# Attention with beacon keys and an ELU feed-forward on one Trainium2 core: a planner's order replaced by tables of order, engines and buffers, with batch 0's keys and queries loaded in two parts

## The chip, the cores and the metric

The kernel runs on one core of a Trainium2 chip. Its engines are TensorE (matrix products; PE in the profile, PEld for its weight loads), VectorE (DVE), ScalarE (ACT), GpSimd (POOL) and SyncE (SP, which only issues DMAs here). Each engine works through its own list of instructions in order and waits on semaphores for what other engines or DMAs have finished. The metric is device microseconds of one execution: the median of 3 runs before is 353.73 us (353.72 to 354.24).

## The reference

For 8 batches and 8 heads, with 576 queries of 64 elements, 16 beacon keys and values that every query sees, and a causal mask over the 576 others; then a feed-forward with ELU over all 4608 tokens:

```python
k_all = concatenate([beacon_k, k], axis=2);  v_all = concatenate([beacon_v, v], axis=2)
scores = matmul(q, k_all.T) / sqrt(64);      scores = where(causal, -1e9, scores)
a = exp(scores - max);                       a /= a.sum(-1) + 1e-09
x = matmul(a, v_all)                         # back to (4608, 512)
h = x @ w_in                                 # 512 -> 2048
g = where(h > 0, h, exp(min(h, 0)) - 1)
out = g @ w_out                              # 2048 -> 512
```

## The kernel before, in words

**Attention.** Heads are taken in pairs (4 pairs a batch, 32 in all). Keys and queries must stand with their 64 elements on the partitions. For batches 0 to 2 a pair's keys and queries are loaded together (L314, 288 KB each), cast to bf16 in one instruction (L323) and transposed by TensorE in ten 128 x 128 pieces (L388, L390; batch 0: L398, L401, into two buffers). Copies then put them in order into kT and qT (L413, L415, L411; L422, L423, L428). Batches 3 to 7 are loaded by token (L340), cast (L346) and transposed by DMA (L353). The scores of a pair are computed in four units (L439), each unit one exponential on ScalarE (L448) with masks by GpSimd on the diagonal pieces (L454). The products with the values (L473) carry a column of ones, whose sum divides the result (L488, L489). The result is turned into xT by TensorE (L499, copy L510) for batches 0 and 1 and by DMA (L359) from batch 2 on.

**Feed-forward.** Tokens go in 11 tiles: 128, 128, 256, then eight of 512. Up: four accumulating matmuls for each 512 columns of output (L529), exponential on ScalarE (L536), clamp on GpSimd (L540), join with max on VectorE (L549). Down: sixteen accumulating matmuls for 128 tokens (L563), a copy (L569), a store (L573). The last 128 tokens are written in two halves. The weights are loaded by GpSimd with a cast on the way (L380), one quarter of a matrix in each DMA.

**Buffers.** PSUM holds two score buffers of two banks (tag sc) and four banks (tag ff) for all else; SBUF has 6 staging buffers of loads (4 of them until batch 1's keys are turned), 3 of casts (2 until then), 8 of exponentials, 18 of feed-forward activations.

**What sets the order.** A planner (class Plan, L27) runs a small model of the engines while the kernel is built: every operation has an engine, a priority key, a duration and the buffers it takes and gives back; at each moment the free engine takes the ready operation with the lowest key for which buffers are there. Keys come from tuned numbers (SHIFT, AT, AT0, PACES and others). Until 30 us of its model, whenever TensorE has nothing ready, the planner puts in a filler: a matmul of ones into a spare bank (L274), which keeps TensorE running. The order found is then written out, so on the chip it is fixed; the fillers are counted out beforehand. A filler's buffer comes from a rotating pool, so most fillers wait for an earlier filler. ScalarE issues 56 loads (half of the token loads, most values), SP the others, all transposes by DMA and the stores; GpSimd issues the 8 loads of weights. The next DMA on SP or ScalarE takes one of 8 semaphores in turn and waits for that one's earlier transfer.

The functions that the change and the prediction touch:

Of the kernel before, what the change touches and what calls it, by code (L numbers as in the profile page):

```python
# [15 lines left out]
P = 128  # L16


class Op:
    def __init__(self, eng, key, dur, fn, deps=(), take=(), give=(), mode=None, lat=0.03, queue=0, parts=1):  # L20
        self.eng, self.key, self.dur, self.fn = eng, key, dur, fn
        self.deps, self.take, self.give = [d for d in deps if d is not None], take, give
        self.mode, self.lat, self.queue, self.parts = mode, lat, queue, parts
        self.left, self.after, self.rest = 0, [], parts


class Plan:  # L27
    MODE_COST = 0.1

    def __init__(self, slots, window):  # L30
        self.slots, self.window, self.ops = dict(slots), window, []

    def add(self, *args, **kw):
        op = Op(*args, **kw)
        self.ops.append(op)
        return op

    def run(self):
        for i, op in enumerate(self.ops):
            op.seq = i  # L40
            op.left = len(op.deps)
            for d in op.deps:
                d.after.append(op)
        ready = {op.eng: [] for op in self.ops}
        pending = {eng: sorted((o.key, o.seq) for o in self.ops if o.eng == eng) for eng in ready}
        done = set()
        first = dict.fromkeys(pending, 0)
        free = dict.fromkeys(pending, 0.0)
        mode, lines, turn = None, ([], [], []), 0

        def arrive(o):
            if o.eng == "DMA":
                lines[o.queue].append(o)
            else:
                heapq.heappush(ready[o.eng], (o.key, o.seq))

        for op in self.ops:
            if not op.left:
                arrive(op)
        events, order, now, n_left, tick = [], [], 0.0, len(self.ops), 0  # L60
        while n_left:
            for eng in ready:
                if free[eng] > now + 1e-9:
                    continue
                if eng == "DMA":
                    if any(lines):
                        turn = next((turn + i) % 3 for i in (1, 2, 3) if lines[(turn + i) % 3])
                        op = lines[turn][0]
                        free[eng] = now + op.dur / op.parts
                        heapq.heappush(events, (free[eng], tick, None))  # L70
                        tick += 1
                        op.rest -= 1
                        if not op.rest:
                            lines[turn].pop(0)
                            heapq.heappush(events, (free[eng] + op.lat, tick, op))
                            tick += 1
                    continue
                line = pending[eng]
                while first[eng] < len(line) and line[first[eng]][1] in done:
                    first[eng] += 1  # L80
                if first[eng] == len(line):
                    continue
                limit = line[first[eng]][0] + self.window.get(eng, 1e9)
                skipped, op = [], None
                while ready[eng]:
                    item = heapq.heappop(ready[eng])
                    o = self.ops[item[1]]
                    if item[0] > limit:
                        skipped.append(item)
# [788 lines left out]
```

## Time and profile before

| what | value |
|---|---|
| median of 3 runs | 353.73 us |
| the profiled execution: span from the first to the last instruction | 352.5 us |
| TensorE busy | 343.3 us (97%), of which fillers 19.1 |
| VectorE, ScalarE, GpSimd busy | 205.8, 194.1, 179.4 us |
| DMA | 52.55 MB, mean 149 GB/s |
| first score matmul, first up-projection matmul | 9.38 us, 31.91 us |

The profile comes from one execution, and its span is 1.2 us under the median of the runs; sums are made against the span. "Busy" of TensorE counts fillers too, and its matmuls overlap each other: where the pace matters, take the difference between two starts. A DMA share above 1 says that packets overlap within the 16 transfer engines.

### The profile page before, as it was taken

Reading aid. Unit: us, or ns where it says so; the run is one execution under the profiler, and the core shown is the slowest. Engines: PE = TensorE matmul, PEld = TensorE weight load, DVE = VectorE, ACT = ScalarE, POOL = GpSimd, SP = SyncE. Lnnn points to the kernel's source line nnn. Section 1 sums busy time; section 2 is a strip of 40 time slices with the busy share of each in tenths; the row PEclk is TensorE's granted clock in tenths of the full one; section 3 lists DMA queues with packets and bytes.
Section 4 is the critical chain, followed back from the end, with each engine's and each line's share of the span. In section 5 each row is a group of like instructions: output and inputs, shape, how many; then the busy total and the mean of one; then the engine's idle time right before and its main releaser. Section 6 shows DMA issues by size and latency. Waiting matters only on the chain.

```text
span 352.5 us, 8440 instructions
## 1 busy us (share of the span) xinstructions
PE 343.3 (97%) x3295; PEld 195.6 (55%) x3295; DVE 205.8 (58%) x428; ACT 194.1 (55%) x289; POOL 179.4 (51%) x353
## 2 busy tenths in 40 slices
PE   8999999999999989999999999999999999999996
PEld 5668887545555445545476664554445544444444
DVE  1478797557556567557746565764665555455322
ACT  2586887577556746684576547663477443343200
POOL 5587776556635655475475455463554333434200
PEclk9999999999999999999999999999999999999999
DMA  7999996798998979899999679767460220000112
GB/s 189 260 286 221 206 238 130 227 215 146 165 209 144 208 153 185 160 195 204 152 232 150 146 138 237 143 104 182 96 144 32 60 69 32 31 31 32 47 72 91
DMA packets 139480, 52.55 MB, mean 149 GB/s; under 512 B 127536, under 2 KB 131888, under 8 KB 139440
## 3 DMA queue, kind: packets, MB, share of 16 engines
q1 hardware_dynamic: 87472, 35.55, 46.7%
q10 hardware_dynamic: 47744, 12.26, 18.9%
q0 software_dynamic: 4224, 4.19, 7.1%
q8 instruction: 26, 0.43, 0.5%
q14 instruction: 14, 0.11, 0.1%
HBM read 37.22 MB, written 9.44 MB: 132 GB/s over the span
## 4 chain that ended last, share of the span: by engine, by line
PE 82%; DMA 7%; DVE 4%; SPq 2%; POOL 1%; issue 1%; ACT 1%; ACTq 0%; POOLq 0%; DVEq 0%
PE ops L563 32%; PE hps L529 32%; PE av L473 8%; PE sc L439 7%; DMA st<-in_k_dram 3%; PE spare L274 3%; DMA st<-in_q_dram 2%; DMA xT<-x 1%; SPq L314 1%; DMA kT<-st 1%; DVE gt L549 1%; POOL et L454 1%; DVE x L489 1%; ACT et L448 1%; POOL e L540 1%
## 5 line engine op out<-in xcount | busy, mean ns | idle before, releaser
L529 PE MATMUL hps<-xT,w_in 128*128 128x512 f16 (+2 forms) x768 | 141.4, 326 | 2.8 <-DVE gt L549 1.3
L563 PE MATMUL ops<-w_out,gt 128*128 128x512 f16 (+1 forms) x592 | 143.9, 374 | 0.0
L549 DVE SCALAR_TENSOR_TENSOR gt<-e,hps 128x512 f16<-128x512 f32 x144 | 97.6, 684 | 74.9 <-POOL e L540 74.5
L540 POOL TENSOR_SCALAR e<-e 128x512 f32<-128x512 f32 x144 | 88.1, 614 | 102.4 <-ACT e L536 100.5
L536 ACT ACTIVATE e<-hps 128x512 f32<-128x512 f32 x144 | 85.6, 600 | 94.3 <-PE hps L529 90.2
L448 ACT ACTIVATE et<-sc 128x768 f16<-128x768 f32 (+3 forms) x128 | 104.1, 863 | 31.8 <-PE sc L439 31.6
L529 PEld LDWEIGHTS <-w_in 128*128 128x128 f16 x768 | 68.0, 98 | 57.6 <-issue 3.6
L563 PEld LDWEIGHTS <-gt 128*128 128x128 f16 x592 | 54.1, 98 | 56.5 <-issue 3.0
L454 POOL TENSOR_SCALAR_AFFINE_SELECT et<-et 128x256 f16<-128x256 f16 (+2 forms) x160 | 61.5, 410 | 44.9 <-ACT et L448 40.8
L473 PEld LDWEIGHTS <-et 128*128 128x128 f16 (+1 forms) x960 | 36.1, 97 | 11.0 <-issue 2.2
L569 DVE COPY osb<-ops 128x512 f32<-128x512 f32 (+1 forms) x37 | 25.0, 675 | 26.2 <-PE ops L563 25.3
L473 PE MATMUL av<-v,et 128*128 128x65 f16 (+1 forms) x960 | 39.7, 193 | 0.3 <-DVE x L489 0.3
L439 PE MATMUL sc<-qT,kT 64*128 64x80 bf16 (+3 forms) x704 | 35.2, 228 | 0.3 <-ACT qT L428 0.2
L489 DVE TENSOR_TENSOR x<-av,rl 128x256 f16<-128x256 f32 (+2 forms) x68 | 32.1, 472 | 2.3
L439 PEld LDWEIGHTS <-kT 64*128 64x128 bf16 x704 | 20.7, 95 | 18.9 <-issue 16.8
L488 DVE RECIPROCAL rl<-av 128x4 f32<-128x4 f32 (+2 forms) x68 | 12.4, 182 | 21.4 <-PE av L473 20.3
L373 DVE CAST v<-vst 128x512 f16<-128x512 f32 (+1 forms) x40 | 21.1, 529 | 4.1 <-DMA vst<-in_v_dram 4.1
L274 PE MATMUL spare<-ones 128*128 128x256 bf16 x111 | 19.1, 304 | 1.6 <-DVE ones L816 1.3
L274 PEld LDWEIGHTS <-ones 128*128 128x128 bf16 x111 | 10.9, 109 | 6.2 <-issue 1.7
L346 DVE CAST st<-st 128x1024 bf16<-128x1024 f32 (+2 forms) x18 | 11.6, 655 | 2.8 <-DMA st<-in_k_dram 1.4
L323 POOL CAST st<-st 128x1152 bf16<-128x1152 f32 x8 | 9.1, 1142 | 5.7 <-DMA st<-in_q_dram 3.9
L346 POOL CAST st<-st 128x1024 bf16<-128x1024 f32 (+2 forms) x12 | 10.7, 892 | 2.0 <-DMA st<-in_k_dram 2.0
(35 smaller groups left out, 68.0 us busy)
## 6 DMA issues: line engine op xcount, KB each, us to landing
out_dram<-osb SPq DMA_DIRECT2D x35, 256.0 KB, 2.6
st<-in_q_dram ACTq DMA_DIRECT2D x20, 256.0 KB, 4.3
vst<-in_v_dram ACTq DMA_DIRECT2D x15, 256.0 KB, 4.1
st<-in_k_dram SPq DMA_DIRECT2D x15, 256.0 KB, 5.0
st<-in_k_dram SPq DMA_DIRECT2D x12, 288.0 KB, 7.1
st<-in_q_dram SPq DMA_DIRECT2D x11, 288.0 KB, 6.9
vst<-in_v_dram SPq DMA_DIRECT2D x9, 256.0 KB, 7.0
w_in<-in_moe_w_in_dram POOLq DMA_DIRECT2D x4, 512.0 KB, 12.7
```

Source lines behind the costliest of these rows:

```text
L274: nc.tensor.matmul(out=spare[:, 0:2 * P], lhsT=ones[:, 0:P], rhs=ones, start=True, stop=True)
L439: nc.tensor.matmul(out=sc[:, h, o:o + w], lhsT=kT[D * h:D * h + D, P * jc:P * jc + P], rhs=qT[D * h:D * h + D, q0:q0 + w], start=True, sto ...
L448: nc.scalar.activation(out=et[:, :, 0:w], in_=scs[n, u][:, :, 0:w], func=AFT.Exp, bias=0.0, scale=float(1.0 / (D ** 0.5)))
L454: nc.gpsimd.affine_select(out=et[:, :, c0:c0 + dw], in_=et[:, :, c0:c0 + dw], compare_op=ALU.is_ge, fill=fill0, base=q0 + NB - P * jc, pat ...
L473: nc.tensor.matmul(out=av[:, c:c + D + 1], lhsT=ets[n, CUT.unit_of[jc, at]][0:m, h, col:col + P], rhs=v16[0:m, jc, 2 * hp + h, 0:D + 1], s ...
L489: nc.vector.tensor_tensor(out=x16s[b % 2][:, blks[0]:blks[0] + nb, P * hp:P * hp + P].rearrange("q i (h d) -> q i h d", d=D), in0=av[:, :, ...
L529: nc.tensor.matmul(out=hps[:, o:o + z - a], lhsT=w_in16[:, cc, P * fc:P * fc + P], rhs=xT[cc][:, a % RING:a % RING + z - a], start=(cc == ...
L536: nc.scalar.activation(out=e, in_=hpss[tt, i], func=AFT.Exp, bias=0.0, scale=1.0)
L540: nc.gpsimd.tensor_scalar(out=e, in0=e, scalar1=1.0, scalar2=0.0, op0=ALU.min, op1=ALU.max)
L549: nc.vector.scalar_tensor_tensor(out=gt, in0=es[tt, i], scalar=1.0, in1=hpss[tt, i], op0=ALU.subtract, op1=ALU.max)
L563: nc.tensor.matmul(out=opss[tt, t4][:, cols], lhsT=gts[tt, fc][:, P * t4:P * (t4 + 1)], rhs=w_out16[:, fc, cols], start=(fc == 0), stop=(f ...
L569: nc.vector.tensor_copy(out=osb[:, slice(*cols)], in_=opss[tt, t4][:, slice(*cols)])
```

## The change

The planner goes. A class Program holds the operations with the engines that each may use and the buffers that each takes and gives back, and three tables say the rest: ORDER, one number for each operation in the order in which they are written out (negative numbers stand for that many fillers); PICKS, a letter for each operation that may run on several engines; PLACES, which buffer each taken one is. Buffers are fixed tiles instead of rotating pools. The tables were made outside the kernel by a planner that took transfers on time and late at once.

Batch 0's keys and queries are loaded, cast, transposed and copied in two parts, tokens 0 to 255 and 256 to 575; the first unit of scores needs only the first part. A unit of scores is one operation (before, two were tied together in most places). The memsets of the beacon buffers and of the exponentials' pads go to VectorE. Which engine casts and copies, and which queue issues a load, is decided by PICKS: ScalarE issues 22 loads instead of 56, SP 233 DMAs instead of 191, GpSimd 8 as before. In the built programs there are 76 fillers instead of 111, the first 15 ahead of the first transpose (before 28).

```diff
-class Plan:
...
-                if op is None:
-                    if eng == "PE" and now < self.fill_until and self.slots["ff"]:
...
+    def run(self, order, picks, places, fill):
+        picks, places, used = iter(picks), iter(places), set()
+        for op in self.ops:
+            if len(op.engines) > 1:
+                op.eng = next(picks)
...
+        for i in order:
+            if i < 0:
+                at = int(next(places), 36)
+                assert ("bank", at) not in used
+                fill(self.rooms["bank"][at])
+                continue
+            op = self.ops[i]
...
+ORDER = [i for t in """
+0 1 12 13 14 90 20 19 -15 15 16 17 18 21 -9 22 26 97 98 51 91 58 52 53 27 23 24 25 -7 30 92 4 32 33 34 35 -1 93
...
+    rooms = {
+        "st": tiles(6, [P, 2, G * D], FP32, "st"),
+        "sb": tiles(3, [P, G, 2, D], BF16, "sb"),
...
+        "bank": [psum.tile([P, 512], FP32, name=f"bank_{i}") for i in range(4)],
+        "pair": [psum.tile([P, 2, 512], FP32, name=f"pair_{i}") for i in range(2)],
...
+    CUTS = (0, 256, S)
+    GS = [(z - a) // HALF for a, z in zip(CUTS, CUTS[1:])]
...
+    def add_pair_halves(n):
...
+        for half in range(2):
+            if half == 0:
+                k_in = st = add("SA", load_k, n, half, take=["st"])
...
+            T = add("P", do_T2, n, half, deps=[cast] + (all_T[b][-1:] if half else [bk_in[b]]), take=["bank"],
+                    give=[(sb, 0)] if half else [])
...
+            need = ready if b else ready[0] + (ready[1] if u else [])
+            SC = add("P", do_SC, n, u, deps=need, take=["pair"])
...
-            nc.gpsimd.memset(t, 0.0)
-            nc.gpsimd.memset(et[:, :, CUT.width[-1]:CUT.width[-1] + P - BLOCKS[-1][1]], 0.0)
+        nc.vector.memset(t, 0.0)
+        nc.vector.memset(et[:, :, WIDTH[-1]:WIDTH[-1] + P - BLOCKS[-1][1]], 0.0)
```

More of the change, by code (lines that the diff above doesn't have):

```diff
@@ L1 @@
-import heapq
-from functools import partial
 from contextlib import ExitStack
@@ L173 @@
     assert G * HALF == S
+    CUTS = (0, 256, S)
+    GS = [(z - a) // HALF for a, z in zip(CUTS, CUTS[1:])]
+    VG = 4
     NKC = -(-SK // P)
@@ new lines, in do_P, with do_Pcopy @@
+    def do_P(e, bank0, bank1, b, half):
+        for g in range(VG):
+            for c, bank in ((2 * half, bank0), (2 * half + 1, bank1)):
+                vps[b, c] = bank
+                rows = slice(32 * c, 32 * c + 32)
+                e.matmul(
+                    out=bank, lhsT=sel[rows, g, :], rhs=vq[rows, :, D * g:D * g + D],
+                    start=(g == 0), stop=(g == VG - 1), skip_group_check=True)
+    def do_Pcopy(e, b, c):
+        copy(e, v16s[b % 2][:, c, :, 0:D], vps[b, c].rearrange("p (h d) -> p h d", h=H))
```

1139 lines of the change are left out of this document (489 added, 650 removed), and 70 rows, old and new, of the table ORDER.

## The prediction

> **What bounds the kernel now.** I read the page first, then the windows, the groups by line, TensorE's timeline and the chain. The page says that TensorE is the engine, and the groups of its lines say how much of that is not work of the reference: the fillers of L274.
>
> ```profile
> PE 343.3 (97%) x3295; PEld 195.6 (55%) x3295; DVE 205.8 (58%) x428; ACT 194.1 (55%) x289; POOL 179.4 (51%) x353
> ...
> L274 PE MATMUL spare<-ones 128*128 128x256 bf16 x111 | 19.1, 304 | 1.6 <-DVE ones L816 1.3
> ```
>
> The span is 352.5. So a planner that only packs TensorE tighter has 352.5 - 343.3 = 9.2 us of idle time and 19.1 us of fillers to win. Where they lie is seen in the windows (columns: stretch and its length, busy us of PE, PEld, DVE, ACT and POOL with counts, granted clock, DMA share, GB/s); 31.9 is the start of the first up-projection matmul:
>
> ```profile
> 0.00:31.90 31.90, 28.91 (x364) 20.91 (x365) 16.36 (x54) 17.58 (x26) 22.10 (x50) 1.00 1.08 238
> 31.90:60.00 28.10, 27.82 (x458) 23.44 (x458) 22.95 (x54) 22.34 (x35) 19.72 (x38) 1.00 1.10 210
> 60.00:260.00 200.00, 197.23 (x1901) 107.21 (x1899) 122.88 (x247) 121.05 (x179) 107.04 (x211) 1.00 0.90 172
> 260.00:352.50 92.50, 89.34 (x578) 44.08 (x576) 43.60 (x75) 33.10 (x52) 30.50 (x56) 1.00 0.16 50
> ```
>
> Idle time of TensorE: 2.99 us up to 31.9, 0.28 to 60, 2.77 to 260, 3.16 to the end, which is the last copy and store. In the built order all fillers stand ahead of 31.9. The first stretch is therefore the only large one: of its 31.9 us, 31.9 - 2.99 - 19.1 = 9.8 us are work. TensorE's timeline (start, length, operation, count) shows its two ends and the pace of the fillers:
>
> ```profile
> 1.26 5.70 PE L274 MATMUL spare<-ones 128*128 128x256 bf16 x28 [1.26 <-DVE ones L816]
> 7.00 0.68 PE L398 MATMUL tr<-identb,st 128*128 128x128 bf16 x9
> ...
> 13.95 2.25 PE L274 MATMUL spare<-ones 128*128 128x256 bf16 x19
> 16.04 0.34 PE L473 MATMUL av<-v,et 128*128 128x65 f16 x6
> ...
> 31.91 1.05 PE L529 MATMUL hps<-xT,w_in 128*128 128x128 f16 x16 [0.54 <-DVE xT L510]
> ```
>
> Twenty-eight fillers took 7.00 - 1.26 = 5.74 us, 0.205 each; later nineteen took 16.04 - 13.95 = 2.09, 0.11 each. After 60 TensorE waits for little; the view of the waits (who for whom, us in total, times, longest) has two rows worth naming, and the chain (start, length, what) shows one of them to begin with a late transfer:
>
> ```profile
> PE hps L529 <- DVE gt L549: 1.3, 2, 0.9
> PE hps L529 <- DMA xT<-x: 0.8, 1, 0.8
> ```
>
> ```profile
> 126.41 3.38 DMA kT<-st
> ...
> 131.45 1.89 PE hps L529 x8
> ```
>
> **The change, part by part.** The work of TensorE is the same: both built programs hold the same matmuls except 76 fillers for 111. The question is the place of the first up-projection and what follows it.
>
> *Fillers and the first stretch.* In the built order of the changed kernel the first L529 group (now L547) stands behind the same 9.8 us of work, behind 72 fillers, and behind 30 changes between score matmuls (64 rows) and others; before there were all 111 fillers and 24 changes. A change of kind costs time:
>
> ```profile
> 157.23 0.81 PE L529 MATMUL hps<-xT,w_in 128*128 128x512 f16 x3
> 157.97 0.52 PE L439 MATMUL sc<-qT,kT 64*128 64x256 bf16 x14
> 158.42 1.04 PE L529 MATMUL hps<-xT,w_in 128*128 128x512 f16 x4
> 159.29 1.03 PE L563 MATMUL ops<-w_out,gt 128*128 128x512 f16 x4
> ```
>
> Four matmuls of 512 columns take 159.29 - 158.42 = 0.87, so three take 0.65; with scores behind them the three took 157.97 - 157.23 = 0.74. I take 0.09 us for each change, into the scores and out of them. Six more are +0.55.
>
> The fillers: 15 stand ahead of the first transpose, 15 x 0.205 = 3.1, and 57 later. At the bare pace these are 57 x 0.11 = 6.3; at the mean of the later 83 before, (19.1 - 5.74) / 83 = 0.161 with their waits in them, 9.2. So the fillers take 9.4 to 12.3 us, and if the idle 2.99 us stay, the first up-projection starts at 9.8 + 0.55 + 2.99 + 9.4 = 22.7 to 25.6. The lower end supposes that every wait falls as the table planned it. I take 25.0, nearer the upper end, since transfers that come late turn into idle time where fillers are counted out beforehand: 31.9 - 25.0 = **-6.9 us**.
>
> Can the other engines follow? ScalarE must get through 16 exponentials of batch 0 ahead of that point; VectorE and GpSimd feed it; w_in must have landed.
>
> ```profile
> L448 ACT ACTIVATE et<-sc 128x768 f16<-128x768 f32 (+3 forms) x128 | 104.1, 863 | 31.8 <-PE sc L439 31.6
> ...
> L454 POOL TENSOR_SCALAR_AFFINE_SELECT et<-et 128x256 f16<-128x256 f16 (+2 forms) x160 | 61.5, 410 | 44.9 <-ACT et L448 40.8
> ```
>
> ```profile
> 9.76 0.78 ACT L448 ACTIVATE et<-sc 128x736 f16<-128x736 f32 x1 [1.17 <-PE sc L439]
> 22.66 3.20 POOL L380 DMA_DIRECT2D w_in<-in_moe_w_in_dram x4
> ```
>
> ```profile
> DMA to landing us min/median/max: 8.2/12.7/17.1
> ```
>
> The last row is of w_in. 16 x 0.863 = 13.8 us from the first exponential, and about 2 us of copies that the new order puts between them. The first exponential began at 9.76, behind a load of 288 KB for each of keys and queries, a cast and a transpose at 7.00. In parts, 4 of 9 columns come first: the cast and the copies shrink with them, and 15 fillers ahead of the transpose (1.26 + 3.1 = 4.4) say when the table wants it. With the first exponential at about 7.3 the last ends at 7.3 + 13.8 + 2 = 23.1 or later. So 22.7 is about the floor, and 25.0 can be kept. The first w_in is issued on GpSimd behind four casts and eight masks instead of at 22.66; eight masks of 0.41 chained behind exponentials put it near 14, and with 8.2 to 12.7 to landing it is there at 22 to 27. This is what is late next: if it is 27, the gain is 4.9.
>
> *The loads in parts.* Eight more DMAs in all, and 42 more on SP's queue: ScalarE issues 22 instead of 56. The bytes are the same. That the pieces of 1024 and 1280 bytes cost the transfer engines more than those of 2304 no row shows; bounded by nothing and by one doubling of the share of batch 0's keys and queries, I take nothing, since the stretch after keeps 1.10 of DMA share anyway and the table has the order of loads in its hand.
>
> *Preparing tiles.* Ten memsets move from GpSimd to VectorE, which had nothing between its own memsets and 7.49:
>
> ```profile
> L823 POOL MEMSET et<- 128x96 f16 x8 | 1.0, 178 | 0.0
> L820 POOL MEMSET bk<- 128x512 bf16 x2 | 1.0, 524 | 0.0
> ```
>
> ```profile
> 7.49 0.49 DVE L413 COPY kT<-tr 128x320 bf16<-128x320 bf16 x1 [5.89 <-PE tr L398]
> ```
>
> Hidden by that wait for the first loads; without the cover 2 us at most, once.
>
> *After the first up-projection.* 148 changes of kind in all for 136; six more lie here: +0.55. Of the 2.77 + 0.28 us of idle time, the 0.8 behind DMA xT<-x and the wait ended at 131.45, which starts with a key transpose, are what a plan with late transfers should lose; bounds -2.8 (all gone) and +3.0 (three more waits like the longest, 0.9). I take **-1.0**.
>
> *The end.* The last group is the same halved tile, one copy and store: 3.16 us, no change.
>
> Sum: -6.9 + 0.55 - 1.0 = -7.35, with the other +0.55 already inside the 25.0. The span goes from 352.5 to 345.15; the median of the runs, 353.73, is 1.2 above this span, so 346.4.
>
> *The clock.* The row of the 28 fillers at 0.205 and that of the 19 at 0.11 are two paces of one instruction; if the paces are 0.21 and 0.11, the slow one held for most of the 28, some 5 us. With 15 fillers ahead of the first transposes, up to ten of the later ones may still be slow: +1.0, which is inside the 25.0. A rule speaks against the change here: the Trainium skill, "TensorE: Matmul & The Clock Gate", Part 1, says that TensorE starts at 1.2 GHz, gets 2.4 GHz after about 3.4 us of sustained work, and falls back after an idle window of that length. By the Trainium skill's 3.4 us the +1.0 would be next to nothing, if no gap comes ahead of the first transpose; the trace's 5 us is longer.
>
> **Rivals.**
> 1. *The table holds to its plan.* Fillers at the bare pace, first up-projection at 22.7, all later waits gone: 352.5 - 9.2 + 0.55 - 2.8 = 341.05, so 342.3. Against it: before, too, 111 fillers at the bare pace (28 x 0.205 + 83 x 0.11 = 14.9) became 19.1.
> 2. *The transfers take it back.* The DMA share stands at 1.08 and 1.10 up to 60 us, so it is full; if weights and batch 1 land when they did, TensorE waits for them and the early start is worth nothing: 352.5 + 1.1 - 1.0 = 352.6, so 353.8, no change. For it: the full share. Against it: TensorE waited only 0.28 us from 31.9 to 60, so the loads were ahead of it.
> 3. *SP's queue becomes single file* (the other side). 42 more loads stand on the queue that also issues the transposes:
>
> ```profile
> L353 SPq DMA_TRANSPOSE kT<-st x25: 1174/1211/2362, 77.3 to 247.1; - x25
> L353 SPq DMA_TRANSPOSE qT<-st x25: 1188/1217/2577, 81.7 to 250.9; - x25
> ```
>
> ```profile
> L359 SPq DMA_TRANSPOSE xT<-x x30: 1183/1251/2437, 101.8 to 285.7; - x30
> ```
>
> ```profile
> 23.75 0.34 SPq L369 DMA_DIRECT2D vst<-in_v_dram x1
> 24.14 1.26 SPq L314 DMA_DIRECT2D st<-in_k_dram x2
> ```
>
>    At 0.34 to 0.63 us each, 42 loads are 14 to 26 us more on SP. Each waits in line for a landing or a free buffer, and behind it wait the transposes of batches 2 to 7 and the stores. If all of it delays a transpose that TensorE needs, the cost is 14 or more: 345.15 + 14 = 359.15, so 360.4. It decides from 7.35 / 6 = 1.2 us a batch. Against it: 80 transposes of 1.2 us are 98 us and the 153 other DMAs 52 to 96, together 150 to 194 of the first 290 us, so SP has room on the mean.
> 4. *The clock stays low.* A wait that no filler covers keeps the slow pace: the 9.8 us of work and the 57 later fillers (6.3) take twice as long, 25.0 + 16 = 41 for the first up-projection, so 352.5 + 9.1 + 0.55 - 1.0 = 361.2 and 362.4. Against it: no wait of TensorE in any row here is over 1.3 us, and the pace, once 0.11, stayed so. The fall back after idle time in the Trainium skill, "TensorE: Matmul & The Clock Gate", Part 1, would make this case; no row here shows one.
>
> **How the numbers follow.** Forecast 0.77, its own range from just above rival 1 to 351.0 (25.6 and +3.0 instead of 25.0 and -1.0: 352.5 - 6.3 + 0.55 + 3.0 = 349.75, so 351.0). Rival 1 0.06, rival 2 0.06, rival 3 0.09, rival 4 0.02. The range of 8 in 10 is 342.3 to 351.0: it holds the forecast and half of rival 1. A measurement of this kernel tells about 0.2% (0.7 us) from no change. Faster: 0.77 + 0.06 = 0.83. Same: 0.06. Slower: 0.09 + 0.02 = 0.11.
>
> **What would show it.** The first L547 matmul near 25; fillers at 10 to 12 us busy; idle time of TensorE from there to 260 at 2 us or less; SP without a wait that ends in TensorE. I am wrong if the first up-projection starts after 28, if TensorE idles more than 4 us between it and 260 behind DMA or behind what a transpose feeds, or if the filler pace is 0.2 after the first transpose.

## The result and the profile after

The changed kernel takes 357.86 us (median of 4 runs, 357.00 to 359.35), the kernel before in the same session 353.90 (353.72 to 354.24): a ratio of 1.0127 (95% interval 1.009 to 1.0165). It is 1.3% slower; the forecast was 346.4. The profiled execution took 358.2, its span is 356.5, 4.0 more than before.

The page (share of the span, instructions) and the group of the fillers:

```profile
PE 342.4 (96%) x3260; PEld 192.3 (54%) x3260; DVE 206.8 (58%) x439; ACT 187.0 (52%) x283; POOL 180.2 (51%) x352
...
L294 PE MATMUL bank<-ones 128*128 128x256 bf16 x76 | 15.2, 321 | 1.3 <-DVE ones L768 1.3
```

TensorE is busy 0.9 us less than before, and its idle time went from 9.2 to 14.1. The windows of the changed kernel, in the same stretches (the last with its own end), say where:

```profile
0.00:31.90 31.90, 28.18 (x387) 19.82 (x388) 20.99 (x79) 17.97 (x26) 17.01 (x39) 1.00 0.96 232
31.90:60.00 28.10, 26.09 (x406) 21.38 (x404) 21.38 (x43) 20.52 (x32) 22.25 (x41) 1.00 1.05 211
60.00:260.00 200.00, 195.32 (x1857) 105.06 (x1856) 116.62 (x234) 110.92 (x167) 104.37 (x205) 1.00 0.93 171
260.00:356.50 96.50, 92.81 (x620) 46.02 (x618) 47.83 (x85) 37.55 (x61) 36.58 (x70) 1.00 0.16 51
```

Idle time is the length less the first number behind it: 2.01 us from 31.9 to 60 (before 0.28), 4.68 to 260 (before 2.77), 3.69 at the end (before 3.16). TensorE's timeline of the start (start, length, operation; in brackets the idle time ahead and what ended it):

```profile
1.26 3.38 PE L294 MATMUL bank<-ones 128*128 128x256 bf16 x15 [1.26 <-DVE ones L768]
6.19 0.61 PE L354 MATMUL bank<-identb,sb 128*128 128x128 bf16 x4 [1.55 <-DVE sb L291]
...
6.70 2.13 PE L294 MATMUL bank<-ones 128*128 128x256 bf16 x9
8.62 0.74 PE L354 MATMUL bank<-identb,sb 128*128 128x128 bf16 x5
9.29 0.49 PE L465 MATMUL pair<-qT,kT 64*128 64x240 bf16 x4
...
28.20 1.07 PE L547 MATMUL bank<-xT,w_in 128*128 128x128 f16 x16
```

The first up-projection starts at 28.20 instead of 31.91. So the start did gain, 3.7 us, and the stretch behind it lost more. In the chain of the changed kernel (start, length, what) the up-projection begins with the landing of the first quarter of w_in, at 28.16:

```profile
18.03 10.13 DMA w_in<-in_moe_w_in_dram
```

TensorE's own list had come there at 28.10, so it waited only 0.1 us for it. In other profiles this wait is longer (see the experiments).

To add up the losses I took, for each matmul, the distance to the next one's start, less the bare pace of its shape (0.216 us for 512 columns, 0.109 for 256, 0.056 for 128) and 0.095 for each change into or out of scores. What is left is waiting, over all of it; the idle times above are smaller, since they leave out the part of a wait in which the matmul ahead is still counted as running. Behind the first up-projection it sums to 5.1 us before and to **11.7** after. Of the 11.7, 1.74 lie at 45 us in one place, 6.0 between 120 and 220 (before 2.0), 0.7 in the last 6 us (before nothing).

The places are seen in single rows. At 45 us TensorE waits for an exponential, which waits for a copy of keys on VectorE; VectorE's rows show four joins of the feed-forward ahead of that copy (its transposes ended at 43.1):

```profile
42.24 2.47 DVE L565 SCALAR_TENSOR_TENSOR gt<-e,bank 128x512 f16<-128x512 f32 x4
44.63 0.82 DVE L291 COPY kT<-pair 128x576 bf16<-128x576 bf16 x2
```

```profile
46.95 0.51 PE L465 MATMUL pair<-qT,kT 64*128 64x240 bf16 x14 [1.68 <-ACT et L474]
```

At 150 us a copy into an output buffer waits for a store that frees the buffer. SyncE's rows (SPq) show the stores behind four transposes:

```profile
139.83 5.13 SPq L515 DMA_TRANSPOSE xT<-x  x4
145.00 0.58 SPq L595 DMA_DIRECT2D out_dram<-osb  x1
145.63 0.43 SPq L395 DMA_DIRECT2D st<-in_k_dram  x1
146.16 0.63 SPq L595 DMA_DIRECT2D out_dram<-osb  x1
```

```profile
149.93 0.69 DVE L591 COPY osb<-bank 128x512 f32<-128x512 f32 x1 [1.36 <-DMA out_dram<-osb]
```

```profile
150.68 1.67 PE L547 MATMUL bank<-xT,w_in 128*128 128x512 f16 x7 [0.98 <-DVE osb L591]
```

And SyncE as a whole: summing the lengths of its DMA rows between 120 and 220 us gives 71.2 us in 68 DMAs before and **94.0 us in 91 DMAs** after, 41 of them transposes in both. At their median lengths (1.26 us a transpose, 0.58 a load or store) the 91 would make 81 us; the other 13 are rows that take longer, and what those wait for the rows don't say. No pause between two of these rows is longer than 0.5 us after; before there are pauses of 3.5, 3.4 and 4.1. Before 120 and behind 220 the two kernels are alike (40.9 and 40.1 from 60 to 120; 29.2 and 28.1 from 220 to 260).

### The profile page after: what moved, and what is told of

Same layout as the page of the kernel before. It is cut to its first block, busy times and chain, and to the rows that moved or that the text cites. A ratio compares the mean times of both kernels' runs of the same rounds, so it can differ in the third digit from the quotient of the medians.

```text
span 356.5 us, 8356 instructions
## 1 busy us (share of the span) xinstructions
PE 342.4 (96%) x3260; PEld 192.3 (54%) x3260; DVE 206.8 (58%) x439; ACT 187.0 (52%) x283; POOL 180.2 (51%) x352
## 4 chain that ended last, share of the span: by engine, by line
PE 65%; DMA 12%; DVE 8%; POOL 7%; SPq 3%; issue 3%; ACT 2%; DVEq 0%; ACTq 0%; POOLq 0%
PE bank L585 30%; PE bank L547 23%; PE bank L495 5%; PE pair L465 5%; DVE gt L565 3%; POOL e L558 3%; DMA w_in<-in_moe_w_in_dram 3%; POOL et L479 3%; DMA w_out<-in_moe_w_out_dram 2%; DMA qT<-sb 2%; DMA st<-in_k_dram 2%; DVE kT L291 1%; ACT et L474 1%; DMA st<-in_q_dram 1%; DVE osb L591 1%
## 5 line engine op out<-in xcount | busy, mean ns | idle before, releaser
L474 ACT ACTIVATE et<-pair 128x800 f16<-128x800 f32 (+3 forms) x128 | 105.6, 867 | 66.6 <-PE pair L465 64.0
L547 PE MATMUL bank<-xT,w_in 128*128 128x512 f16 (+2 forms) x768 | 136.0, 326 | 3.1 <-DVE osb L591 2.0
L585 PE MATMUL bank<-w_out,gt 128*128 128x512 f16 (+1 forms) x592 | 133.7, 373 | 1.6 <-DVE gt L565 0.6
L565 DVE SCALAR_TENSOR_TENSOR gt<-e,bank 128x512 f16<-128x512 f32 x144 | 95.7, 683 | 59.5 <-POOL e L558 58.8
L554 ACT ACTIVATE e<-bank 128x512 f32<-128x512 f32 x144 | 83.3, 602 | 75.5 <-PE bank L547 65.2
L591 DVE COPY osb<-bank 128x512 f32<-128x512 f32 (+1 forms) x37 | 25.0, 675 | 55.0 <-PE bank L585 32.7
L495 PE MATMUL bank<-v,et 128*128 128x65 f16 (+1 forms) x960 | 38.6, 193 | 0.8 <-POOL et L479 0.3
L465 PE MATMUL pair<-qT,kT 64*128 64x80 bf16 (+3 forms) x704 | 36.2, 229 | 2.3 <-ACT et L474 2.0
L509 DVE TENSOR_TENSOR x<-bank,rl 128x256 f16<-128x256 f32 (+2 forms) x68 | 32.1, 471 | 2.3
L508 DVE RECIPROCAL rl<-bank 128x4 f32<-128x4 f32 (+2 forms) x68 | 12.4, 182 | 15.9 <-PE bank L495 15.3
L294 PE MATMUL bank<-ones 128*128 128x256 bf16 x76 | 15.2, 321 | 1.3 <-DVE ones L768 1.3
```

Of the source, the lines that this page charges most:

```text
L294: nc.tensor.matmul(out=bank[:, 0:2 * P], lhsT=ones[:, 0:P], rhs=ones, start=True, stop=True)
L465: e.matmul(out=pair[:, h, o:o + w], lhsT=kT[D * h:D * h + D, P * jc:P * jc + P], rhs=qT[D * h:D * h + D, q0:q0 + w], start=True, stop=True ...
L474: e.activation(out=et[:, :, 0:w], in_=scs[n, u][:, :, 0:w], func=AFT.Exp, bias=0.0, scale=float(1.0 / (D ** 0.5)))
L495: e.matmul(out=av[:, c:c + D + 1], lhsT=ets[n, unit_of[jc, at]][0:m, h, col:col + P], rhs=v16s[b % 2][0:m, jc, 2 * hp + h, 0:D + 1], start ...
L509: e.tensor_tensor(out=x16s[b % 2][:, blks[0]:blks[0] + nb, P * hp:P * hp + P].rearrange("q i (h d) -> q i h d", d=D), in0=av[:, :, :, 0:D] ...
L547: e.matmul(out=bank[:, o:o + z - a], lhsT=w_in16[:, cc, P * fc:P * fc + P], rhs=xTa[:, cc, a % RING:a % RING + z - a], start=(cc == 0), st ...
```

## The experiments

Three theories: **A**, SyncE's single file makes transposes, loads and stores late (rival 3 of the prediction, smaller); **B**, the fixed order puts on VectorE or GpSimd an operation that TensorE doesn't need ahead of one that it does; **C**, the weights or what else the start waits for are late. All edits are on the changed kernel. The table has each kernel's median, its ratio to the kernel before (interval), and from its one profile the start of the first up-projection, the waits from 120 to 220 us and all waits behind the first up-projection, counted as above. The medians come from several sessions, so the ratios are what to compare.

| kernel | us | ratio | first up-projection | waits 120-220 | all later waits |
|---|---|---|---|---|---|
| changed | 357.86 | 1.0127 (1.009-1.0165) | 28.20 | 6.0 | 11.7 |
| e1_osb4 | 358.12 | 1.0094 (1.006-1.0127) | 28.34 | 5.1 | 10.5 |
| e2_stores_first | 376.75 | 1.0661 (1.0562-1.0761) | 27.87 | 6.0 | 28.8 |
| e3_w_in_early | 361.29 | 1.0187 (1.0108-1.0266) | 29.72 | 5.0 | 10.8 |
| e4_loads_act | 366.18 | 1.0322 (1.024-1.0403) | 30.24 | 5.8 | 19.4 |
| e5_fill24 | 360.86 | 1.018 (1.0126-1.0234) | 28.12 | 9.3 | 15.3 |
| e7_order | 356.01 | 1.0034 (1.0004-1.0065) | 29.93 | 6.1 | 9.7 |
| e9_score_first | 358.19 | 1.0102 (1.0032-1.0172) | 30.32 | 6.0 | 12.6 |
| e10_stores_pool | 362.61 | 1.0224 (1.0187-1.0262) | 30.15 | 2.9 | 13.1 |
| e11_casts | 355.21 | 1.0027 (0.9998-1.0056) | 28.99 | 5.1 | 9.3 |
| e12_stores_act | 352.60 | 0.9956 (0.9933-0.9978) | 29.28 | 1.5 | 5.5 |
| e13_both | 352.18 | 0.9961 (0.9937-0.9985) | 27.61 | 3.1 | 7.3 |
| e14_fill_gap | 350.96 | 0.9928 (0.99-0.9956) | 27.58 | 1.3 | 4.6 |
| e15_stores_act_alone | 356.28 | 1.0041 (1.0009-1.0073) | 29.59 | 1.5 | 8.1 |
| e16_gap_alone | 358.17 | 1.0115 (1.0064-1.0166) | 27.62 | 5.4 | 12.4 |
| e17_vector_relief | 359.91 | 1.0156 (1.0112-1.02) | 30.67 | 5.3 | 11.5 |

The first up-projection is itself not steady: in the ten profiles whose edits don't touch what stands ahead of it (changed, e1, e2, e4, e7, e10 to e13, e15) it lies between 27.61 and 30.24. In each of them TensorE's list has come to it 0.1 to 1.5 us earlier, and the landing of the first quarter of w_in ends the wait. In e7:

```profile
27.97 0.43 PE L529 MATMUL bank<-identh,x 80*128 80x80 f16 x5
29.93 1.07 PE L552 MATMUL bank<-xT,w_in 128*128 128x128 f16 x16 [1.54 <-DMA w_in<-in_moe_w_in_dram]
```

So waits are compared place by place, times by the ratios, and a shift of the start by less than 2.6 us in one profile says little.

### SyncE's single file

**e1**: a fourth output buffer, the one freed longest ago taken next.

```diff
-        "osb": tiles(3, [P, DM], FP32, "osb"),
+        "osb": tiles(4, [P, DM], FP32, "osb"),
+                if room == "osb":
+                    at = self.spare.pop(0)
```

> The changed kernel with four output buffers instead of three, taken in the order in which they came free. Theory A (SP's single file: stores stand behind transposes, and VectorE waits for an output buffer): VectorE's three idle stretches of 7.3 us ahead of L591 go, and with them TensorE's waits of about 2.9 us near 148, 150, 184 and 187; the time falls from 357.9 to 354.5 to 355.5. Theory B (VectorE, GpSimd and ScalarE have casts and copies ahead of joins in their fixed lists, SP does not decide): the waits stay, 357 to 358.5. Theory C (weights late at the start) expects 357 to 358.5 as well.

The time did not fall by the 2.4 to 3.4 us of theory A. The waits at 148 to 150 and 184 went as far as they hung on output buffers, but new ones came: at 157 (0.83) behind a cast that waits for its load, at 207 (1.38) behind a transpose, and at 196 (1.01) behind a cast whose own wait the profile doesn't explain. So the buffer was one place where lateness showed, and not what made it.

**e2**: each store is issued directly behind its copy.

```diff
+    for i, op in enumerate(plan.ops):
+        if op.fn is do_store:
+            order.insert(order.index(i - 1) + 1, i)
```

> The changed kernel with each store put in the order directly behind its copy, so ahead of the transposes that stood between. Theory A: as with a fourth buffer, 354.5 to 355.5, unless a store at the head of SP's list holds back the transposes while it waits for its copy; then up to 358. Theory B and C: 357 to 358.5.

The time is 6.6% above the kernel before. SyncE stands at the store until the copy is done, and loads and transposes stand behind it; the view of the waits has SyncE waiting for these copies:

```profile
SPq L595 <- DVE osb L591: 116.3, 20, 24.8
```

This is 116.3 us in 20 waits, where the changed kernel has 82.0 in 13. So the table was right to set stores late, and a DMA that waits on SyncE costs what stands behind it. The same kernel shows the clock: behind a gap of 4.62 us four matmuls of 512 columns take 1.86 instead of 1.03 us (granted clock 0.53 from 96 to 103.3):

```profile
93.12 1.03 PE L547 MATMUL bank<-xT,w_in 128*128 128x512 f16 x4
98.77 1.86 PE L547 MATMUL bank<-xT,w_in 128*128 128x512 f16 x4 [4.62 <-DVE osb L591]
```

**e10**: all stores on GpSimd's queue, in their places.

```diff
-                    add("S", do_store, p, t4, c0, c1, deps=[o], give=[(o, 0)])
+                    add("G", do_store, p, t4, c0, c1, deps=[o], give=[(o, 0)])
```

> The change, with all stores issued from GpSimd's queue in the places that the table has for them, instead of SyncE's; 37 DMAs of 0.78 us by the rows of its weight loads, 29 us on an engine that is busy for 180 of 356. Theory A (stores and transposes in one file): the waits at 148 to 150, 159 and 184 go (2.9 of the 11.7) and loads issue earlier; the time falls by 1 to 3 us where GpSimd has room. Theory B (order on the engines): those go, but clamps and masks behind the stores' issue wait 0.8 us each time, 37 times; new waits of 0.2 to 0.5 at the places where a clamp is next: the late waits stay at 10 to 16 and the time at 357 to 362.

From 120 to 220 the waits fell from 6.0 to 2.9, as theory A has it. But at 101 GpSimd stood 2.78 us at a store whose copy was late, and masks stood behind it (TensorE waits 1.55); and at 263 TensorE waits 2.3 us for a copy whose output buffer a store frees that GpSimd, behind masks, had issued only at 261.92. The file was moved to another engine.

```profile
101.67 0.58 POOL L595 DMA_DIRECT2D out_dram<-osb  x1 [2.78 <-DVE osb L591]
102.27 0.75 POOL L479 TENSOR_SCALAR_AFFINE_SELECT et<-et 128x256 f16<-128x256 f16 x2
```

**e4**: query loads of batches 3 to 7 and value loads of 3 to 6 on ScalarE, where the kernel before has many of them.

```diff
+                if op.fn.__name__ in ("load_tok", "load_tok2") and not op.args[1] or op.fn.__name__ == "load_v" and op.args[0] in (3, 4, 5, 6):
+                    op.eng = "A"
```

> The changed kernel with the query loads of batches 3 to 7 and the value loads of batches 3 to 6 on ScalarE's queue, as before the change; the order is kept. Theory A: SP has about 35 DMAs fewer ahead of stores and transposes, the 7.3 us stretches of VectorE shrink, 354 to 356. Theory B: no gain, 357 to 358.5, or slower, up to 361, where a load that waits for a buffer holds back ScalarE's exponentials.

It is worse than either theory had it. A load that stands behind ScalarE's exponentials is issued when ScalarE gets there; in the chain one is issued at 85.6 and lands 6.91 later, at 92.55. VectorE has stood at its cast for 4.30 us, and the copy that frees a bank for TensorE stands behind the cast:

```profile
92.64 0.42 DVE L403 CAST sb<-st 64x512 bf16<-64x512 f32 x1 [4.30 <-DMA st<-in_q_dram]
92.98 0.68 DVE L593 COPY osb<-bank 128x512 f32<-128x512 f32 x1
```

```profile
93.71 1.70 PE bank L549 x4
```

**e15**: only stores that ScalarE need not wait for go to ScalarE: 13 of the 37, those that the table puts several ScalarE operations behind their copy. Nothing else.

```diff
+LATE = [1023, 1001, 1149, 1143, 1155, 1231, 1243, 1237, 1325, 1331, 1319, 1401, 1407]
...
+        for i in LATE:
+            self.ops[i].eng = "A"
```

> The changed kernel with the 13 late stores issued by ScalarE instead of SyncE, and nothing else. Theory A (SyncE's single file holds most of the later waits from 120 to 215): of the 11.7 us of late waits the 6.2 from 120 to 220 fall to 2 or less, those at 45 (1.74), 49 to 94 (2.0) and 350 (0.68) stay; late waits 7 to 8 us, the time 3.5 to 5 us less than the change's 357.9, ratio about 1.000. Theory B (order on VectorE and GpSimd, for which the moved stores only helped together with the repaired order): late waits stay above 9.5.

As theory A expected: 8.1 us of waits in all, 1.5 from 120 to 220. The window of that stretch, changed kernel and then e15:

```profile
120.00:220.00 100.00, 96.16 (x948) 54.49 (x946) 59.63 (x119) 56.65 (x87) 53.49 (x106) 1.00 0.95 179
```

```profile
120.00:220.00 100.00, 99.52 (x990) 56.59 (x988) 63.67 (x127) 59.94 (x93) 55.70 (x110) 1.00 1.10 189
```

TensorE's idle time there is 3.84 us and 0.48 (1.25 in the kernel before); the DMA share rises from 0.95 to 1.10, so the transfers had room. By the ratios the time is 0.9% less than the changed kernel's, some 3 us, a little under the 3.5 to 5 expected. That the start of this profile is 1.4 us later is not the reason: e7 starts at 29.93 and keeps 6.1 us of waits in this stretch, e14 starts at 27.58 and has 1.3. SyncE's rows still fill 90.7 us, with 7 DMAs fewer inside, but there are pauses again (1.0 us at 208, 5.6 at 217). So a small relief was enough; why so little is enough, no run shows.

### The order on the engines

The edits of e7, e9, e11 and e16 move operations while the kernel is built; where a diff shows numbers of operations, it is the order before and behind the edit, and not the code.

**e7** (on e1): VectorE's copy of keys ahead of two joins; at the end, the last tile's first half ahead of the last quarter of the tile before, so that its copy has matmuls beside it.

```diff
-1032 1033 1034 1035 984 985 986 987 261 262 263
+1032 1033 1034 984 985 986 261 262 1035 987 263
...
-1763 1764 1766 1767 1768 1770 1771 1772
+1766 1767 1768 1763 1764 1770 1771 1772
```

> The kernel with four output buffers, and two places of the table put in another order: the key copy of batch 1's last pair ahead of two joins on VectorE (43.4 instead of 44.6), and at the end the last tile's first half ahead of the fourth quarter of the tile before, so that its copy lies beside matmuls. Theory B (a fixed order on VectorE that stands an op which TensorE needs behind two that it doesn't): the wait of 1.74 us at 45 becomes 0.4 to 0.8, the wait of 0.68 at 350 goes, the rest stays; time 1.5 to 2.0 us under that with four output buffers (358.1 beside a before of 354.8), so a ratio of 1.004 to 1.006. Theory A (SyncE's single file is the whole of it): these two places change, but what follows waits that much longer for transfers: no more than 0.5 us is left of it by 260 us.

The wait of 1.74 became 0.55 and that at the end went. In the profile of e7 the same scores as at 46.95 above:

```profile
47.48 0.51 PE L470 MATMUL pair<-qT,kT 64*128 64x240 bf16 x14 [0.49 <-ACT et L479]
```

The two places are worth 1.9 us of waits, and they were theory B's. The stretch from 120 to 220 kept its 6.1.

**e11** (on e7): two token casts, which stood on VectorE ahead of joins while their loads were late, put behind those joins, and two transposes of keys behind two of xT.

```diff
-1155 639 649 640 641 642 511 1260 1261 1262 1263 612 1248 1244 1245 1246 586 587
+1155 649 511 1260 1261 1262 1263 612 1248 1244 1245 1246 586 587 639 640 641 642
...
+    move([760], behind=1363)
+    move([762, 761, 763], behind=737)
```

> The kernel with the two places put in another order (four output buffers), and two token casts on VectorE, which stood ahead of joins while their loads were late (157 and 196), put behind those joins; the second one's two key transposes on SyncE go behind the two transposes of xT that TensorE waited for at 208. Theory B (order on VectorE): the waits at 158 (0.80) and 196 (1.02) go, and that at 208 (1.95) falls below 0.5; late waits 9.7 to 6 to 7, time 3 us less than the kernel it starts from, beside its start as it falls (28.2 or 30). Theory A (SyncE is always busy from 118 to 215 and every load and transpose is as late as before): the waits move to the next load or transpose; late waits stay at 8.5 to 10.

The waits named went or shrank (208: 1.95 became two of 0.32 and 1.25), and others came in their place: 1.55 at 151, where the next cast on VectorE waits for its load, and 0.85 at 227. 9.3 us for 9.7, and the ratio is the same as e7's: theory A.

```profile
151.46 0.69 DVE L406 CAST sb<-st 128x1024 bf16<-128x1024 f32 x1 [2.63 <-DMA st<-in_k_dram]
```

**e12** (on e7): the 13 stores of e15 on ScalarE.

> The kernel with the two places put in another order, and 13 of the 37 stores issued by ScalarE instead of SyncE, those that the table sets 7 or more ScalarE operations behind their copy, so that ScalarE need not wait for them. SyncE loses 13 issues of 0.6 us, 8 us between 100 and 260. Theory A (single file): loads and transposes from 118 to 215 come up to 6 us earlier by the end of it, the waits at 123, 132 to 134, 158, 185, 196 and 208 (5.6 in all) fall below 2.5; ScalarE pays 13 x 0.4 beside its 187 us. Theory B: they stay at 4.5 or more.

The waits from 120 to 220 fell to 1.5, all later waits from 9.7 to 5.5, about what the kernel before has, and the ratio is 0.9956: faster than before.

**e13**: e11 and e12 in one.

> Both: the casts behind the joins and the 13 stores on ScalarE. If the two causes are separate, late waits fall to 4 to 5 us (before has 5.1), and with the start at 28.2 the span is 348 to 350; ratio 0.985 to 0.995. If one makes the other needless, late waits as in the better of the two.

7.3 us of waits, not 4 to 5; one of them, 1.0 at 55, is the landing of w_out. The casts add nothing that shows once SyncE is relieved.

### The start

**e3**: the first load of w_in is issued ahead of the later casts on GpSimd (operation 972 behind the cast of pair 1's first part).

> The changed kernel with the first quarter of w_in issued by GpSimd ahead of the masks and the value cast, so at about 9 to 10 us instead of 18. Theory C (the start is set by the landing of w_in at 28.2): the first up-projection moves from 28.2 to 25.5 to 26.5 and the time falls by about 2 to 355.5 to 356.5. If later waits absorb what the start wins (theory A or B alone), the first up-projection moves and the time stays at 357 to 358.5.

The first up-projection came at 29.72, not earlier, and TensorE has no wait for w_in ahead of it any more. The chain of this kernel goes through a value load that took 8 us:

```profile
10.58 8.00 DMA vst<-in_v_dram
```

So an earlier w_in alone brings nothing in this profile: TensorE's list comes to the up-projection late. Part of that is the clock (granted 0.88 from 10 to 30 us, in the changed kernel 1.00), so this isn't a clean test. For the changed kernel itself theory C is worth the 0.1 us that TensorE waits for w_in there, and in the other profiles up to 1.5.

**e5**: the fillers behind the first 24 are left out (they compute nothing that is used).

```diff
+        n += i < 0
+        if i >= 0 or n <= 24:
+            order.append(i)
```

> The change, with its 52 fillers behind the first 24 left out (they compute nothing that is used). Theory S1 (the start is set by the chain of loads, casts, copies and exps; fillers only fill it): the first up-projection stays at 28.2 +- 0.5, TensorE idle before it grows by the time of those fillers (6 to 8 us), the late waits stay at 11.7, time 357 to 360 unless the clock falls. Theory S2 (fillers stand ahead of work that is ready, since the table planned them for later loads): the first up-projection comes 1 to 4 us earlier and the time falls to 354 to 357. Rival on the clock: with gaps of several us the matmuls behind them run at twice their pace for some 4 us, as behind the gaps of the kernel with each store behind its copy; then the first up-projection comes later than 28.7.

The first up-projection stayed at 28.12. From 1.26 us to there TensorE's idle time grew from 2.3 to 5.7 us, and the granted clock fell from 1.00 to 0.87 (0.83 from 9.3 to 20 us). So the fillers fill time in which little else is ready, as S1 has it, and they keep the clock up; a gain that the lower clock took back isn't excluded by this profile. Later the kernel had more waits (9.3 from 120 to 220).

**e9**: the first unit of scores ahead of the second half's transposes, four fillers ahead of it, three behind, two behind the transposes.

```diff
--9 22 26
+-4 26 -3 22 -2
```

> The change, with the first unit of scores of pair 0 put ahead of the transposes of that pair's second half (it needs the first half alone), two of the fillers between moved behind them. Theory S1a (the two parts bring nothing because the table sets the first score behind the second half's transposes, 9.29 instead of some 7.9): first score at 7.8 to 8.0, first exp at 8.3 to 8.5 and the first up-projection 0.5 to 1.4 us earlier, the time with it. Theory S1b (the start is set later, by the row of casts, copies and exps of the other pairs up to 28): first score at 7.8 to 8.0 all the same, and the first up-projection where it was, 28.2 +- 0.3.

Here the reason shows. ScalarE's timeline:

```profile
7.72 0.78 ACT L474 ACTIVATE et<-pair 128x736 f16<-128x736 f32 x1 [5.63 <-PE pair L465]
11.52 1.72 ACT L474 ACTIVATE et<-pair 128x768 f16<-128x768 f32 x2 [3.01 <-PE pair L465]
```

The first exponential came 2.1 us earlier than in the changed kernel (9.82), and then ScalarE waited 3.01 us, since the next units need the second half: second exponential at 11.52, before the edit at 11.18. (Nine fillers ahead of these units took 2.13 us in this profile, with a granted clock of 0.88 up to 10 us.) Loading in parts brings one exponential of sixteen forward. TensorE's list came to the first up-projection at 28.43, not earlier than in the changed kernel, and then waited for w_in.

**e16**: 23 fillers instead of 15 ahead of the first transposes.

```diff
--15 15
+-23 15
```

> The changed kernel with 23 fillers instead of 15 ahead of the first transposes, and nothing else. Theory K (the gap of 1.55 us keeps the clock's warm-up back): the first transposes' matmuls and the fillers behind them go at 0.11 instead of 0.213, the waits up to the first up-projection fall from 1.6 to 0.9 and it starts 0.5 to 1.0 earlier; times 356 to 357.5. Rival L (what is behind waits for a load and its cast on GpSimd in any case): the first up-projection stays at 28.2 +- 0.4 and the time at 357.5 to 358.5.

```profile
1.26 4.25 PE L294 MATMUL bank<-ones 128*128 128x256 bf16 x23 [1.26 <-DVE ones L768]
5.34 0.39 PE L354 MATMUL bank<-identb,sb 128*128 128x128 bf16 x4
...
5.62 1.15 PE L294 MATMUL bank<-ones 128*128 128x256 bf16 x9
8.04 0.45 PE L354 MATMUL bank<-identb,sb 128*128 128x128 bf16 x5 [1.27 <-POOL sb L291]
```

The nine fillers behind the first transposes take 1.15 instead of 2.13. That this is the gap's doing is not shown: e1, with the 15 fillers and a gap of 1.69 us, has the same pace (e2, e3 and e4 too):

```profile
6.18 0.40 PE L359 MATMUL bank<-identb,sb 128*128 128x128 bf16 x4 [1.69 <-DVE sb L296]
6.47 1.15 PE L299 MATMUL bank<-ones 128*128 128x256 bf16 x9
```

Nor does the pace decide: the second half's transposes, at 8.04 instead of 8.62, now wait 1.27 us for their cast on GpSimd, as rival L has it. The first exponential comes at 8.80 and the first up-projection at 27.62; the kernels with 15 fillers in the old order have 8.97 to 10.16 and 27.61 to 30.67, so neither is clear of their spread. At 57 us a quarter of w_out has not landed when TensorE gets there,

```profile
57.34 1.02 PE L585 MATMUL bank<-w_out,gt 128*128 128x512 f16 x4 [1.07 <-DMA w_out<-in_moe_w_out_dram]
```

and the span is 356.5 as before the edit; the ratio is the changed kernel's within its interval.

**e17** (on e5): four casts between 16 and 22 us by ScalarE instead of VectorE.

> The kernel without the 52 later fillers, and four casts between 16 and 22 us (three of values, one of batch 0's last pair) by ScalarE instead of VectorE. Theory V (VectorE's list, gapless from 18.7 to 28.9, sets the start): the first up-projection comes at 26.0 to 27.3 instead of 28.1. Rival X (the row of exponentials on ScalarE, to which these casts add 2 us, or the order of TensorE's own list sets it): 28.0 or later, up to 30.

30.67, but the granted clock was 0.54 from 20 us up to there in this run, so the later start can be the clock's as well as ScalarE's. Whether VectorE or ScalarE holds the stretch from 11 to 28 us stays open.

### Stores, order and fillers together

**e14**: e13 with the fillers of e16.

> Both, and 8 more fillers ahead of the first transposes (23 instead of 15), so that TensorE has no gap of 1.5 us there. Theory K (the gap sets the clock's warm-up back: in the change the 9 fillers behind the gap still take 0.213 each, in before 0.11 from 6.35 on): the fillers behind the first transposes take 0.11, the second half's transposes come 0.3 to 0.9 us earlier, and the first up-projection 0 to 1.0 earlier than without. Rival: the warm-up counts from the first transposes or the load sets it all, then nothing moves.

350.96 us, ratio 0.9928 (0.99 to 0.9956) to the kernel before, where the changed kernel has 1.0127: faster than both. Beside e13 (0.9961, 0.9937 to 0.9985) the intervals overlap, so what the fillers add is not shown. Page and windows of its profile:

```profile
PE 340.3 (98%) x3268; PEld 192.0 (55%) x3268; DVE 207.0 (59%) x439; ACT 186.9 (54%) x283; POOL 179.8 (52%) x352
```

```profile
0.00:27.58 27.58, 24.15 (x332) 17.10 (x332) 18.48 (x70) 15.18 (x22) 15.94 (x37) 1.00 0.91 229
27.58:60.00 32.42, 31.50 (x500) 25.54 (x501) 25.37 (x58) 23.48 (x36) 24.07 (x45) 1.00 1.15 228
...
120.00:220.00 100.00, 99.65 (x969) 56.13 (x967) 62.76 (x124) 58.58 (x90) 54.21 (x108) 1.00 1.08 183
```

Against the changed kernel, waits behind the first up-projection fall by 7.1 us and the span by 7.7.

## Why the prediction was wrong

| step | forecast | measured |
|---|---|---|
| first up-projection | -6.9 | -3.7 |
| six changes of kind behind it | +0.55 | +0.55 (counted in the trace, at 0.095 each) |
| four fillers behind it | not in the sum | +0.4 (at 0.11 each) |
| later waits | -1.0 | +6.6 |
| sum | -7.35 | +3.9 (span +4.0) |

- **"Later waits -1.0" failed**, in sign and size: it is +6.6. This step alone takes the whole gain (with it put right the sum would be +0.65); the smaller gain at the start makes it a loss. Even in TensorE's idle time from 31.9 to 260, which shows less, it is 3.05 us before and 6.69 after: +3.6, beyond the bound of +3.0. The row of before that I read (a transfer at 126 us) gave hope, and nothing of the new order was priced. Shown by e15, and once more by e12 beside e7: some 4.5 us of the waits from 120 to 220 go when 13 stores leave SyncE's file. Shown by e7: 1.9 us are two places of the order, one on VectorE, one at the end ("3.16 us, no change" became 3.69).
- **Rival 3 was the right mechanism, and the argument against it was wrong.** It said that SyncE has room on the mean, 150 to 194 of 290 us. That sum was low (SyncE's rows come to 222 us), and above all the file isn't loaded evenly: in the 100 us from 120 to 220 its rows fill 94.0 us, against 71.2 before. A mean over a stretch three times as long hides that. Its price, 14 us, was too high; what takes up the rest, no run shows. Moving 13 of 233 DMAs takes most of these waits away. The Trainium skill, "DMA: Bandwidth & Descriptors", section "Issuing engines are not separate DMA queues", says that issuing from several engines only saves the issuer's time, which is usually small beside the DMA. The measurement bounds that "usually": SyncE's rows filled 94 of 100 us here, and moving some to ScalarE saved 4.5 us of waits.
- **"First up-projection, -6.9" was mis-sized**: 3.7, and the term that was too small is "the same 9.8 us of work". Counted from start to next start, what isn't a filler takes 12.5 us in the kernel before and 13.2 in the changed one, against 9.8 + 0.55 in the sum. The 9.8 came of taking the fillers' busy time, 19.1, off the stretch; but a filler is still counted as busy when the next matmul has begun, and by starts the 111 fillers took 18.2. The other terms held: the 72 fillers took 12.2 us (forecast 9.4 to 12.3), and the idle 2.99 us became 2.8 (1.26 at the start, 1.55 ahead of the first transposes). So 2.9 of the 3.2 us between 25.0 and 28.2 are this term.
- **The check on the other engines was too low as well.** The first exponential was set at 7.3 and came at 9.82, since the table sets it behind the second half's transposes; e9 shows that even at 7.72 it would bring only one exponential. Nor did the smaller parts land earlier: the first cast starts at 5.71 here, when queries issued second on ScalarE's queue, at 1.60, have landed, and at 5.80 before, with 288 KB issued first, at 0.83. The two casts, of after and of before:

```profile
5.71 0.43 DVE L291 CAST sb<-st 128x512 bf16<-128x512 f32 x1 [3.10 <-DMA st<-in_q_dram]
```

```profile
5.80 1.14 POOL L323 CAST st<-st 128x1152 bf16<-128x1152 f32 x1 [2.03 <-DMA st<-in_q_dram]
```

From the first exponential to the end of the fifteenth, the last that is done ahead of the up-projection, it is 16.6 us (9.82 to 26.38), against 13.8 + 2 for sixteen in the forecast; that part nearly held. "What is late next" named w_in, rightly: it was issued at 18.03 instead of near 14 and landed at 28.16, behind the 27 that the forecast allowed, and the up-projection could not have begun before that, however short the list. Which of VectorE, ScalarE and the loads sets TensorE's own list to 28.1 stays open (e3, e5, e9, e17).
- **"The clock, +1.0"** came true in this profile: the first 24 fillers ran at the slow pace, nine of them behind the gap, some 1.0 us more (2.13 for 1.15). In e1 to e4, with the same 15 fillers ahead, those nine ran fast, so it was one of two outcomes and not a sure term. What the gap has to do with it, e16 doesn't show.
- **Rival 4** did not come to pass in the changed kernel (granted clock 1.00 in every window), but e2, e4 and e5 show the fall of the clock that no row of before showed.
- **Rival 2**: transfers took nothing back as a whole; the share was free to rise from 0.95 to 1.10 in e15. Single transfers do bound the start: w_in, as said, and w_out, for which TensorE waits 1.07 us in e16.

## What to carry to other kernels

When a change moves DMAs to one queue, add up that queue's rows in short windows, here of 100 us, and not over the whole span. Here a window with 94 us of rows (81 at median lengths) made loads, transposes and stores late, and one with 71 did not. A store that was copied long ago can go to any engine's queue for the price of its issue; a DMA that still has to wait holds everything behind it on that engine. An order planned outside is worth checking against its first profile: two small moves were worth 1.9 us of 6.6. And when a sum is made of a pipelined engine's time, take starts and not busy times: the 9.8 us here were 12.5.

## What the runs showed of the hardware

- The clock falls behind gaps, not always of the same length, and sometimes only after the gap. Behind 2.65 us (e4, four matmuls of 512 columns in 1.70), 3.20 (e5, 1.87) and 4.62 (e2, 1.86) matmuls ran at about half pace at once. Behind 2.31 us (e4, at 232.63) the first four still took 1.02, and then the granted clock was 0.50 from 234 to 237 (eight in 3.39 us instead of 1.9); behind 1.89 us (e9, at 30.32) it was 0.50 from 31.5 to 34.9. Behind 3.25 us (e2, at 241.17) it did not fall (granted 1.00 from 236 to 250). The Trainium skill, "TensorE: Matmul & The Clock Gate", Part 1, says that the window of some 3.4 us runs freely, whenever the kernel starts; a limit that isn't sharp fits that, though 1.89 and 2.31 are shorter than the window.

```profile
234.22 3.39 PE L587 MATMUL bank<-w_out,gt 128*128 128x512 f16 x8
```

- The slow pace at the start lasts differently long in kernels with the same opening: nine fillers behind 15 others and a gap took 2.13 us in the changed kernel (gap 1.55) and 1.15 in e1 (1.69). The granted clock, 1.00 in both, doesn't show it; the fillers' pace does.
- Kernels that differ only behind the first up-projection begin it between 27.61 and 30.24 us, in each of ten profiles directly behind the landing of one 512 KB transfer, the first quarter of w_in (its row in the changed kernel: issued at 18.03, 10.13 us on the way).
